# Attention decode: values matmuls in a counted loop on TensorE, one buffer ring for K and V

## Chip, cores and metric

The kernel runs on one core of one Trainium2 chip. The metric is the device time of one execution in microseconds. A profile of one execution shows the engines: PE (TensorE matmuls), PEld (its weight loads), DVE (VectorE), ACT (ScalarE), POOL (GpSimd), SP (the queue that issues the loads), and the DMA transfers.

## The reference: one query per head against 4096 keys

```python
B, H, Sq, Skv, Dh = 8, 32, 1, 4096, 128          # q, k, v in bf16
scale = q.shape[-1] ** -0.5
scores = einsum('bhqd,bhkd->bhqk', q, k) * scale
attn = softmax(scores, axis=-1)
out = einsum('bhqk,bhkd->bhqd', attn, v)
```

There are 256 heads, and each has one query row. K and V are 268 MB each, and every byte of them is used once.

## The kernel before

**Tiles.** A tile t is 8 heads (G) of K or V, and there are 32 tiles (NT). A head's 4096 rows lie on 16 partitions with 256 rows (C) on each, so that a tile of K or V is 128 partitions x 256 rows x 128 numbers, 8.4 MB. Each comes by one DMA (`load`, L139), a few at the two ends of the run in pieces (`cuts`).

**Scores.** `product` (L174) multiplies a quarter of K's rows in place by the query on DVE (L179), and then folds the 128 products to 64 (L182) and, in the first two quarters, to 32 (L187). `sum_over_d` (L194) adds further on PE, by matmuls with an identity, 4 or 8 for a quarter, into one of three PSUM buffers `ps`. `scores_of` (L208) adds the last 8 numbers of each row on DVE (L211). There are four quarters u = 0 to 3 in each tile.

**Weights.** `weights_of` (L218) takes the largest score of the tile's heads, and ACT computes eight exponentials (L240), one for each head's column g: `w[:, c, g]` is the weight of row c in the column of head g, and zero on the partitions of other heads.

**Values.** `values_of` (L250) does 64 matmuls for a tile. Each takes four rows (CB) at once: the stationary operand is w of these rows, 4 x 8 = 32 columns, and the moving operand is 4 x 128 = 512 numbers of V. The 32 output rows go to one of four column groups of PE, `c0 // CB % TG`, so four matmuls in turn write to four quarters of the partitions of `av`. Only the diagonal blocks of the result matter. `copy_of` (L289) copies `av` to SBUF on ACT, and `result_of` (L295) picks the right blocks out of it and adds them up by four matmuls with `pick`, a matrix of zeros and ones that POOL makes at the start (L108 to L123, among the constants). `norm_of`, `recip_of` and `finish_of` divide by the sum of the weights and write out.

**Buffers.** K has two buffers (`k_pool`) and V one (`v_pool`); the last V takes one of K's. So K of tile t+1 waits until K of t-1 is used up, and V of tile t until the values matmuls of t-1 have read V of t-1. The tile framework places all these waits.

**Order.** The order on each engine is written by hand, in the loop at the end (`manual_schedule`). The values matmuls of tile t-1 stand in the middle of tile t, behind the second quarter's sum, with their copy; for the last two tiles they stand behind the fourth quarter's sum. The program is unrolled: every matmul is an instruction of its own, together with a load of its weights.

```python
            if t + 1 < NT:
                load("k", t + 1)
            load("v", t)
            product(t, 0, Q)
            sum_over_d(t, 0)
```

Of the kernel before, what the change touches and what calls it, by code (L numbers as in the profile page):

```python
# [7 lines left out]
ACT = mybir.ActivationFunctionType  # L8
ALU = mybir.AluOpType
AX = mybir.AxisListType  # L10
BF16 = mybir.dt.bfloat16
F32 = mybir.dt.float32

G = 8
KB, VB = 2, 1
TG = 4
R = 2
OB = 4
LAST = 4
NEG = -1.0e30  # L20


@with_exitstack
def kernel(
# [7 lines left out]
    nc = tc.nc  # L32
    B, H, Sq, D = q.shape
    S = k.shape[2]
    P = nc.NUM_PARTITIONS
    assert Sq == 1 and D == 128
    NH = B * H
    PH = P // G
    C = S // PH
    NT = NH // G  # L40
    scale = float(D) ** -0.5
    UC = 64
    DS = 512 // UC
    NU = C // UC
    MC = UC
    CB = 4
    RG = R * G
    NQ = NT // R
    TB = 32
    AG = CB * G  # L50
    assert TG * AG == P and NH % P == 0 and P % G == 0 and TB % PH == 0 and C % CB == 0

    q_n = q.rearrange("b h o d -> (b h o) d").rearrange("(x p) d -> p x d", p=P)
    o_n = out.rearrange("b h o d -> (b h o) d").rearrange("(n u x) d -> n x u d", u=OB, x=RG)
    k_t = k.rearrange("b h s d -> (b h s) d").rearrange("(t p c) d -> t p c d", p=P, c=C)
    v_t = v.rearrange("b h s d -> (b h s) d").rearrange("(t p c) d -> t p c d", p=P, c=C)

    k_pool = ctx.enter_context(tc.tile_pool(name="k_pool", bufs=KB))
    v_pool = ctx.enter_context(tc.tile_pool(name="v_pool", bufs=VB))
    consts = ctx.enter_context(tc.tile_pool(name="consts", bufs=1))  # L60
    q_pool = ctx.enter_context(tc.tile_pool(name="q_pool", bufs=2))
    w_pool = ctx.enter_context(tc.tile_pool(name="w_pool", bufs=2))
    sc_pool = ctx.enter_context(tc.tile_pool(name="sc_pool", bufs=1))
    small = ctx.enter_context(tc.tile_pool(name="small", bufs=2))
    o_pool = ctx.enter_context(tc.tile_pool(name="o_pool", bufs=1))
    ps_s = ctx.enter_context(tc.tile_pool(name="ps_s", bufs=3, space=bass.MemoryType.PSUM))
    ps_v = ctx.enter_context(tc.tile_pool(name="ps_v", bufs=2, space=bass.MemoryType.PSUM))
# [9 lines left out]
        out=ident[:], in_=ident[:], pattern=[[-1, P]], compare_op=ALU.not_equal,  # L77
        fill=1.0, base=0, channel_multiplier=1,
# [31 lines left out]
    for j in range(TG):  # L110
        part = pick[j * AG : (j + 1) * AG, :, :, :]
        nc.gpsimd.affine_select(
            out=part, in_=part, pattern=[[-G, CB], [G, R], [-1, RG]],
            compare_op=ALU.not_equal, fill=1.0, base=0, channel_multiplier=1,
        )
        nc.gpsimd.affine_select(
            out=part, in_=part, pattern=[[-G, CB], [0, R], [0, RG]],
            compare_op=ALU.is_ge, fill=0.0, base=0, channel_multiplier=1,
        )
        nc.gpsimd.affine_select(  # L120
            out=part, in_=part, pattern=[[G, CB], [0, R], [0, RG]],
            compare_op=ALU.is_ge, fill=0.0, base=G - 1, channel_multiplier=-1,
        )  # L123
    ones = consts.tile([P, 1], F32, name="ones")
    nc.vector.memset(ones[:], 1.0)
# [2 lines left out]
    nc.gpsimd.memset(w_last[:], 0.0)  # L128

    loads = {}  # L130
    cuts = {
        ("k", 0): [C // 2] * 2,
        ("k", NT - 3): [C // 2] * 2,
# [4 lines left out]

    def load(kind, t):  # L139
        src = k_t if kind == "k" else v_t  # L140
        home = "v" if kind == "v" and t < NT - 1 else "k"
        pool = k_pool if home == "k" else v_pool
        buf = pool.tile([P, C, D], BF16, name=f"{kind}t", tag=home)
        c0 = 0
        for n in cuts.get((kind, t), [C]):
            nc.sync.dma_start(buf[:, c0 : c0 + n, :], src[t, :, c0 : c0 + n, :])  # L146
            c0 += n
            if kind == "k" and t == 0 and c0 == n:
                nc.sync.dma_start(q_all[:], q_n)
        assert c0 == C  # L150
        loads[kind, t] = buf
# [56 lines left out]
    def scores_of(t, u):  # L208
        if u == 0:
            scs[t] = sc_pool.tile([P, C], F32, name="sc", tag="sc")  # L210
        nc.vector.tensor_reduce(  # L211
            out=scs[t][:, u * UC : (u + 1) * UC], in_=sums.pop((t, u))[:], axis=AX.X, op=ALU.add
        )

    ws = {}
    esums = {}

    def weights_of(t):  # L218
        sc = scs.pop(t)
        pmax = small.tile([P, 1], F32, name="pmax", tag="pmax")  # L220
        nc.vector.tensor_reduce(out=pmax[:], in_=sc[:], axis=AX.X, op=ALU.max)  # L221
        spread = small.tile([P, TB], F32, name="spread", tag="spread")
        nc.vector.tensor_scalar(  # L223
            out=spread[:], in0=same[:], scalar1=pmax[:, 0:1], scalar2=-scale,
            op0=ALU.add, op1=ALU.mult,
        )
        nmax = small.tile([P, 1], F32, name="nmax", tag="nmax")
        nc.vector.tensor_reduce(  # L228
            out=nmax[:], in_=spread[:], axis=AX.X, op=ALU.min, apply_transpose=True
        )  # L230
        bias = small.tile([P, G], F32, name="bias", tag="bias")
        nc.vector.tensor_scalar(  # L232
            out=bias[:], in0=own[:], scalar1=nmax[:, 0:1], scalar2=None, op0=ALU.add
        )
        w = w_pool.tile([P, C, G], BF16, name="w", tag="w")
        if t % R == 0:
            esums[t // R] = small.tile([P, R, G], F32, name="esum", tag="esum")
        esum = esums[t // R]
        for g in range(G):
            nc.scalar.activation(  # L240
                out=w[:, :, g], in_=sc[:], func=ACT.Exp, bias=bias[:, g : g + 1], scale=scale,
                accum_out=esum[:, t % R, g : g + 1],
            )
        ws[t] = w
        if t == NT - 1:
            nc.gpsimd.tensor_copy(out=w_last[:, :, RG - G : RG], in_=w[:, C - LAST : C, :])

    avs = {}

    def values_of(t, lo, hi):  # L250
        vt = loads["v", t]
        w = ws[t]
        if lo == 0:
            avs[t] = ps_v.tile([P, CB * D], F32, name="av", tag="av")
        end = C if t < NT - 1 else C - LAST


        group = [
            0 if t == NT - 1 and C // 2 <= c0 < C // 2 + 3 * C // 16 else c0 // CB % TG
            for c0 in range(0, end, CB)  # L260
        ]
        for c0 in range(lo, hi, CB):
            i = c0 // CB
            j = group[i]
            nc.tensor.matmul(  # L265
                avs[t][j * AG : (j + 1) * AG, :], lhsT=w[:, c0 : c0 + CB, :],
                rhs=vt[:, c0 : c0 + CB, :], start=(i < TG), stop=(j not in group[i + 1 :]),
            )

    ops = {}  # L270
# [16 lines left out]
    combs = {}  # L287

    def copy_of(t):  # L289
        comb = small.tile([P, CB, D], BF16, name="comb", tag="comb")  # L290
        av = avs.pop(t)[:].rearrange("p (m d) -> p m d", d=D)
        nc.scalar.activation(out=comb[:], in_=av, func=ACT.Copy)  # L292
        combs[t] = comb

    def result_of(t):  # L295
        n, r = divmod(t, R)
        comb = combs.pop(t)
        if r == 0:
            ops[n] = ps_o.tile([RG, D], F32, name="op", tag="op")
        if t == NT - 1:  # L300
            for i in range(LAST):
                nc.tensor.matmul(
                    ops[n][:], lhsT=w_last[:, i, :], rhs=loads["v", t][:, C - LAST + i, :],
                    start=False, stop=False,
                )
        for m in range(CB):
            nc.tensor.matmul(  # L307
                ops[n][:], lhsT=pick[:, m, r, :], rhs=comb[:, m, :],
                start=(r == 0 and m == 0), stop=(r == R - 1 and m == CB - 1),
            )  # L310

# [10 lines left out]
            nc.scalar.dma_start(o_n[s, :, lo : u + 1, :], stages[s][:, lo : u + 1, :])  # L322

    Q = C // 4
    load("k", 0)
    with tc.manual_schedule():
        q_prep(0)
        for t in range(NT):
            v_last = t >= NT - 2
            n = t // R - 1  # L330
            if t + 1 < NT:
                load("k", t + 1)
            load("v", t)
            product(t, 0, Q)
            sum_over_d(t, 0)
            if t > 2 and t % R == 1:
                recip_of(n)
                finish_of(n)
            if t + 1 < NT:
                q_prep(t + 1)  # L340
            product(t, Q, 2 * Q)
            sum_over_d(t, 1)
            scores_of(t, 0)
            if t > 0 and not v_last:
                values_of(t - 1, 0, C)
                copy_of(t - 1)
            product(t, 2 * Q, 3 * Q)
            sum_over_d(t, 2)
            scores_of(t, 1)
            product(t, 3 * Q, C)  # L350
            sum_over_d(t, 3)
            scores_of(t, 2)
            if t > 0 and v_last:
                values_of(t - 1, 0, C)
            scores_of(t, 3)
            weights_of(t)
            if t > 0:
                if v_last:
                    copy_of(t - 1)
                if t % R == 0:  # L360
                    norm_of(n)
                result_of(t - 1)
        values_of(NT - 1, 0, C // 2)
        norm_of(NQ - 1)
        recip_of(NQ - 1)
        values_of(NT - 1, C // 2, C - LAST)
        copy_of(NT - 1)
        result_of(NT - 1)
        finish_of(NQ - 1)

# [29 lines left out]
```

## Time and profile before

| | |
|---|---|
| median of 10 runs | 1253.27 us (1252.81 to 1253.87) |
| the profiled execution | 1252.88 us, span 1251.1 us |
| DVE busy | 1038.0 us, 83% |
| PE busy | 504.4 us, 40%, 3067 matmuls |
| ACT busy | 343.8 us, 27% |
| mean granted TensorE clock | 0.635 |
| HBM read | 536.94 MB, 429 GB/s over the span |

The page lists groups of instructions by source line with the number of executions, their busy time and mean, and then the idle time of the engine ahead of them and what ended it. Durations of matmuls overlap, and the busy time of a group counts the overlapped time once. DMA queues are listed with packets, megabytes and the share of the 16 DMA engines' span that they filled. Queues named "instruction" bring the engines' programs.

### The profile page before, as it was taken

What the parts mean: (1) busy time and instruction counts of PE and PEld (TensorE: products, weight loads), DVE (VectorE), ACT (ScalarE), POOL (GpSimd) and SP (SyncE); (2) the same over time, 40 slices, a digit from 0 to 9 for tenths busy, and PEclk for the clock granted to TensorE, in tenths of its full rate; (3) what the DMA queues carried; (4) which work ended last, traced back from release to release, by engine and by line L of the source; (5) the groups of instructions that cost most, each with busy time, mean ns of one, the idle gap of its engine ahead of it and who ended that gap; (6) DMA issues with size and microseconds to landing.
All of it is one profiled execution on the core that took longest, in us unless ns stands there. A gap on an engine that the chain in (4) does not pass through costs nothing.

```text
span 1251.1 us, 7723 instructions
## 1 busy us (share of the span) xinstructions
PE 504.4 (40%) x3067; PEld 176.6 (14%) x3067; DVE 1038.0 (83%) x588; ACT 343.8 (27%) x625; POOL 6.0 (0%) x26
## 2 busy tenths in 40 slices
PE   1344432344333443333533344432444334454455
PEld 0011110111111111111111111111111111111122
DVE  5989898888988889788898888987879888899981
ACT  0321233321233312333123331233321333213333
POOL 1000000000000000000000000000000000000000
PEclk9767655666656666566665666656666556667776
DMA  9999999999999999999999999999999999999997
GB/s 404 436 434 435 436 434 434 434 434 434 434 422 434 436 436 430 430 432 432 437 436 428 435 434 432 424 434 434 436 434 434 437 432 436 432 423 427 429 441 328
DMA packets 11444, 537.50 MB, mean 430 GB/s; under 512 B 1808, under 2 KB 2064, under 8 KB 2320
## 3 DMA queue, kind: packets, MB, share of 16 engines
q1 hardware_dynamic: 11072, 536.94, 99.4%
q8 instruction: 24, 0.39, 0.1%
q10 hardware_dynamic: 336, 0.07, 0.0%
q14 instruction: 12, 0.10, 0.0%
HBM read 536.94 MB, written 0.07 MB: 429 GB/s over the span
## 4 chain that ended last, share of the span: by engine, by line
DMA 76%; PE 14%; DVE 8%; issue 1%; SPq 0%; ACT 0%
DMA vt<-in_v_dram 75%; PE av L265 13%; DVE kt L179 5%; DVE kt L182 2%; PE ps L199 1%; DMA q_all<-in_q_dram 1%; DVE kt L187 0%; DVE sc L211 0%; SPq L146 0%; DVE pmax L221 0%; DVE spread L223 0%; DVE nmax L228 0%; ACT comb L292 0%; PE op L307 0%; ACT stage L316 0%
## 5 line engine op out<-in xcount | busy, mean ns | idle before, releaser
L179 DVE TENSOR_TENSOR kt<-kt,qb 128x8192 bf16<-128x8192 bf16 x128 | 565.1, 4415 | 88.3 <-DMA kt<-in_k_dram 76.8
L199 PE MATMUL ps<-kt,ident 128*128 128x512 bf16 x792 | 295.2, 532 | 661.5 <-DVE kt L187 504.0
L240 ACT ACTIVATE w<-sc,bias 128x256 bf16<-128x256 f32 x256 | 301.0, 1590 | 365.2 <-DVE bias L232 365.2
L182 DVE TENSOR_TENSOR kt<-kt 128x4096 bf16<-128x4096 bf16 x128 | 293.3, 2292 | 4.4
L199 PEld LDWEIGHTS <-ident 128*128 128x128 bf16 x792 | 92.5, 120 | 824.5 <-issue 674.5
L265 PE MATMUL av<-vt,w 128*32 128x512 bf16 x2047 | 181.2, 525 | 43.7 <-DMA vt<-in_v_dram 43.7
L211 DVE TENSOR_REDUCE sc<-ps 128x64 f32<-128x512 f32 x128 | 87.6, 685 | 89.4 <-PE ps L199 89.4
L292 ACT ACTIVATE comb<-av 128x512 bf16<-128x512 f32 x32 | 19.7, 616 | 411.8 <-PE av L265 411.8
L240 ACT ACTIVATION_READ_ACCUMULATOR w<-sc,bias 128x1 f32 x256 | 126.9, 496 | 0.0
L265 PEld LDWEIGHTS <-w 128*32 128x32 bf16 x2047 | 68.0, 127 | 167.8 <-issue 81.4
L187 DVE TENSOR_TENSOR kt<-kt 128x2048 bf16<-128x2048 bf16 x58 | 71.0, 1225 | 2.0
L162 ACT ACTIVATE qg<-qh 8x128 bf16<-8x128 f32 x32 | 8.5, 267 | 93.1 <-PE qh L158 93.1
L307 PE MATMUL op<-comb,pick 128*16 128x128 bf16 x128 | 16.8, 276 | 13.0 <-ACT comb L292 13.0
L221 DVE TENSOR_REDUCE pmax<-sc 128x1 f32<-128x256 f32 x32 | 13.4, 420 | 1.1
L285 DVE RECIPROCAL rz<-zp 16x1 f32<-16x1 f32 x16 | 2.4, 149 | 13.9 <-PE zp L277 13.9
L158 PE MATMUL qh<-q_all,ident 128*8 128x128 bf16 x32 | 8.5, 265 | 13.2 <-DMA q_all<-in_q_dram 13.2
L164 PE MATMUL qp<-qg,heads 8*128 8x128 bf16 x32 | 8.3, 258 | 12.7 <-ACT qg L162 12.7
L307 PEld LDWEIGHTS <-pick 128*16 128x16 bf16 x128 | 9.5, 106 | 25.2 <-issue 25.1
L316 ACT ACTIVATE stage<-op,rz 16x128 bf16<-16x128 f32 x16 | 6.2, 386 | 23.1 <-DVE rz L285 17.0
L166 ACT ACTIVATE qb<-qp 128x128 bf16<-128x128 f32 x32 | 8.9, 278 | 11.0 <-PE qp L164 11.0
L223 DVE TENSOR_SCALAR spread<-same,pmax 128x32 f32<-128x32 f32 x32 | 7.7, 241 | 1.1
L232 DVE TENSOR_SCALAR bias<-own,nmax 128x8 f32<-128x8 f32 x32 | 7.4, 230 | 1.1
(27 smaller groups left out, 26.9 us busy)
## 6 DMA issues: line engine op xcount, KB each, us to landing
kt<-in_k_dram SPq DMA_DIRECT2D x7, 4096.0 KB, 34.2
kt<-in_k_dram SPq DMA_DIRECT2D x2, 2048.0 KB, 36.8
vt<-in_v_dram SPq DMA_DIRECT2D x1, 4096.0 KB, 39.7
vt<-in_v_dram SPq DMA_DIRECT2D x1, 2048.0 KB, 44.2
vt<-in_v_dram SPq DMA_DIRECT2D x1, 1024.0 KB, 46.1
vt<-in_v_dram SPq DMA_DIRECT2D x1, 512.0 KB, 46.9
vt<-in_v_dram SPq DMA_DIRECT2D x31, 33.1
kt<-in_k_dram SPq DMA_DIRECT2D x28, 43.5
```

The costliest lines, as they stand in the source:

```text
L158: nc.tensor.matmul(qh[:], lhsT=ident[:, p0 : p0 + G], rhs=q_all[:, x, :], start=True, stop=True)
L166: nc.scalar.activation(out=qb[:, 0, :], in_=qp[:], func=ACT.Copy)
L179: nc.vector.tensor_tensor(out=part, in0=part, in1=qb[:].to_broadcast([P, MC, D]), op=ALU.mult)
L182: nc.vector.tensor_tensor(out=part[:, :, 0 : D // 2], in0=part[:, :, 0 : D // 2], in1=part[:, :, D // 2 : D], op=ALU.add,)
L187: nc.vector.tensor_tensor(out=part[:, :, 0 : D // 4], in0=part[:, :, 0 : D // 4], in1=part[:, :, D // 4 : D // 2], op=ALU.add,)
L199: nc.tensor.matmul(ps[:], lhsT=ident[:], rhs=kt[:, u * UC : (u + 1) * UC, s * DS : (s + 1) * DS], start=(s == 0), stop=(s == n - 1),)
L211: nc.vector.tensor_reduce(out=scs[t][:, u * UC : (u + 1) * UC], in_=sums.pop((t, u))[:], axis=AX.X, op=ALU.add)
L221: nc.vector.tensor_reduce(out=pmax[:], in_=sc[:], axis=AX.X, op=ALU.max)
L240: nc.scalar.activation(out=w[:, :, g], in_=sc[:], func=ACT.Exp, bias=bias[:, g : g + 1], scale=scale, accum_out=esum[:, t % R, g : g + 1],)
L265: nc.tensor.matmul(avs[t][j * AG : (j + 1) * AG, :], lhsT=w[:, c0 : c0 + CB, :], rhs=vt[:, c0 : c0 + CB, :], start=(i < TG), stop=(j not i ...
L292: nc.scalar.activation(out=comb[:], in_=av, func=ACT.Copy)
L307: nc.tensor.matmul(ops[n][:], lhsT=pick[:, m, r, :], rhs=comb[:, m, :], start=(r == 0 and m == 0), stop=(r == R - 1 and m == CB - 1),)
```

## The change

**Layout of the weights.** w becomes `[P, C // CB, G, CB]`: four rows of one head lie side by side, so that the 32 columns of one values matmul are ordered by head and then by row, and one stretch of 32 numbers serves each matmul. The pattern of `pick` follows and needs one select for each column group in place of three. `w_last`, the copy of the last four rows' weights, is filled through a permuted view.

**Loop.** The values matmuls of all but the last three tiles stand in a new function `values_loop`. The first and last two of the 64 (EDGE) are written out; the other 60 run as ten turns of a loop on PE with six matmuls each (LOOP), whose addresses come from two registers. All 64 write to the first column group, so only 32 partitions of `av` are filled, copied and picked from. A loop is a block of its own in the program: [...]PE waits ahead of it for everything that stands before it in the program. To keep that short, the loop of tile t-1 stands behind the fourth quarter's sum of tile t, and the loads of K t+1 and V t and the fourth reduction of tile t are put behind it in the program (`behind_loop` fixes this order, without a wait). The copy of `av` moves behind the exponentials of tile t.

**Buffers.** K and V share one ring of three buffers. By the order of the loads, K of t+1 takes the buffer of V of t-2, and V of t that of K of t. The score buffer gets a second copy, `comb` loses one.

```diff
-KB, VB = 2, 1
+SLOTS = 3
+LOOP = 6
+EDGE = 2
...
-    k_pool = ctx.enter_context(tc.tile_pool(name="k_pool", bufs=KB))
-    v_pool = ctx.enter_context(tc.tile_pool(name="v_pool", bufs=VB))
+    kv_pool = ctx.enter_context(tc.tile_pool(name="kv_pool", bufs=SLOTS))
...
-    sc_pool = ctx.enter_context(tc.tile_pool(name="sc_pool", bufs=1))
+    sc_pool = ctx.enter_context(tc.tile_pool(name="sc_pool", bufs=2))
...
-            out=part, in_=part, pattern=[[-G, CB], [G, R], [-1, RG]],
+            out=part, in_=part, pattern=[[-1, CB], [CB * G, R], [-CB, RG]],
             compare_op=ALU.not_equal, fill=1.0, base=0, channel_multiplier=1,
-        )
-        nc.gpsimd.affine_select(
-            out=part, in_=part, pattern=[[-G, CB], [0, R], [0, RG]],
-            compare_op=ALU.is_ge, fill=0.0, base=0, channel_multiplier=1,
-        )
-        nc.gpsimd.affine_select(
-            out=part, in_=part, pattern=[[G, CB], [0, R], [0, RG]],
-            compare_op=ALU.is_ge, fill=0.0, base=G - 1, channel_multiplier=-1,
         )
...
+    def behind_loop(made):
+        if loops:
+            tc.add_manual_dep(
+                made.ins, loops[-1].name,
+                mybir.DependencyInfo(
+                    mybir.DependencyClass.NoSync, mybir.DependencyReason.SCHED_ONLY
+                ),
+            )
...
-        home = "v" if kind == "v" and t < NT - 1 else "k"
-        pool = k_pool if home == "k" else v_pool
-        buf = pool.tile([P, C, D], BF16, name=f"{kind}t", tag=home)
+        buf = kv_pool.tile([P, C, D], BF16, name=f"{kind}t", tag="kv")
...
-            nc.sync.dma_start(buf[:, c0 : c0 + n, :], src[t, :, c0 : c0 + n, :])
+            dma = nc.sync.dma_start(buf[:, c0 : c0 + n, :], src[t, :, c0 : c0 + n, :])
+            behind_loop(dma)
...
+        if u == NU - 1:
+            behind_loop(made)
...
-        w = w_pool.tile([P, C, G], BF16, name="w", tag="w")
+        w = w_pool.tile([P, C // CB, G, CB], BF16, name="w", tag="w")
...
+        sc_g = sc[:].rearrange("p (i m) -> p i m", m=CB)
         for g in range(G):
             nc.scalar.activation(
-                out=w[:, :, g], in_=sc[:], func=ACT.Exp, bias=bias[:, g : g + 1], scale=scale,
+                out=w[:, :, g, :], in_=sc_g, func=ACT.Exp, bias=bias[:, g : g + 1], scale=scale,
...
+    def values_loop(t):
+        vf = loads["v", t][:].rearrange("p c d -> p (c d)")
+        wf = ws[t][:].rearrange("p i g m -> p (i g m)")
+        avs[t] = ps_v.tile([P, CB * D], F32, name="av", tag="av")
+        av = avs[t][0:AG, :]
+        nv, nw = CB * D, CB * G
+        def one(i, **how):
+            pe.matmul(
+                av, lhsT=wf[:, i * nw : (i + 1) * nw], rhs=vf[:, i * nv : (i + 1) * nv], **how
+            )
+        with tc.tile_critical() as loop:
+            for i in range(EDGE):
+                one(i, start=(i == 0), stop=False)
+            end = (NV - EDGE) * nw
+            pe.reg_mov(rw, EDGE * nw)
+            pe.reg_mov(rv, EDGE * nv)
+            with pe.While(lambda: pe.snap(rw, min_val=EDGE * nw, max_val=end) < end):
+                ow = pe.snap(rw, min_val=EDGE * nw, max_val=end - LOOP * nw)
+                ov = pe.snap(rv, min_val=EDGE * nv, max_val=(NV - EDGE - LOOP) * nv)
+                for i in range(LOOP):
+                    pe.matmul(
+                        av, lhsT=wf[:, bass.ds(ow + i * nw, nw)],
+                        rhs=vf[:, bass.ds(ov + i * nv, nv)],
+                        start=False, stop=False,
+                    )
+                pe.reg_add(rw, rw, LOOP * nw)
+                pe.reg_add(rv, rv, LOOP * nv)
+            for i in range(NV - EDGE, NV):
+                one(i, start=False, stop=(i == NV - 1))
+        loops.append(loop)
+    LT = NT - 3
...
-        comb = small.tile([P, CB, D], BF16, name="comb", tag="comb")
+        comb = o_pool.tile([P, CB, D], BF16, name="comb", tag="comb")
         av = avs.pop(t)[:].rearrange("p (m d) -> p m d", d=D)
-        nc.scalar.activation(out=comb[:], in_=av, func=ACT.Copy)
+        n = AG if t < LT else P
+        nc.scalar.activation(out=comb[0:n, :, :], in_=av[0:n, :, :], func=ACT.Copy)
...
+            loop = 0 < t <= LT
...
-            if t + 1 < NT:
-                load("k", t + 1)
-            load("v", t)
+            if not loop:
+                if t + 1 < NT:
+                    load("k", t + 1)
+                load("v", t)
...
             scores_of(t, 0)
-            if t > 0 and not v_last:
-                values_of(t - 1, 0, C)
-                copy_of(t - 1)
             product(t, 2 * Q, 3 * Q)
...
             scores_of(t, 2)
-            if t > 0 and v_last:
+            if loop:
+                values_loop(t - 1)
+                load("k", t + 1)
+                load("v", t)
+            if v_last:
                 values_of(t - 1, 0, C)
             scores_of(t, 3)
             weights_of(t)
             if t > 0:
-                if v_last:
-                    copy_of(t - 1)
+                copy_of(t - 1)
```

More of the change, by code (lines that the diff above doesn't have):

```diff
@@ L50 @@
     AG = CB * G
-    assert TG * AG == P and NH % P == 0 and P % G == 0 and TB % PH == 0 and C % CB == 0
+    NV = C // CB
+    assert (NV - 2 * EDGE) % LOOP == 0
+    assert LAST == CB and TG * AG == P and NH % P == 0 and P % G == 0 and TB % PH == 0 and C % CB == 0
     q_n = q.rearrange("b h o d -> (b h o) d").rearrange("(x p) d -> p x d", p=P)
@@ L130 @@
     loads = {}
+    loops = []
+    def behind_loop(made):
[6 more added lines that the diff above has]
+            )
     cuts = {
@@ L210, in scores_of @@
             scs[t] = sc_pool.tile([P, C], F32, name="sc", tag="sc")
-        nc.vector.tensor_reduce(
+        made = nc.vector.tensor_reduce(
             out=scs[t][:, u * UC : (u + 1) * UC], in_=sums.pop((t, u))[:], axis=AX.X, op=ALU.add
         )
+        if u == NU - 1:
+            behind_loop(made)
     ws = {}
@@ L245, in weights_of @@
         if t == NT - 1:
-            nc.gpsimd.tensor_copy(out=w_last[:, :, RG - G : RG], in_=w[:, C - LAST : C, :])
+            nc.gpsimd.tensor_copy(
+                out=w_last[:, :, RG - G : RG].rearrange("p m g -> p g m"),
+                in_=w[:, (C - LAST) // CB, :, :],
+            )
     avs = {}
+    pe = nc.tensor
+    rv = pe.alloc_register("rv")
+    rw = pe.alloc_register("rw")
+    def values_loop(t):
[22 more added lines that the diff above has]
+                        start=False, stop=False,
+                    )
+                pe.reg_add(rw, rw, LOOP * nw)
[4 more added lines that the diff above has]
+    LT = NT - 3
     def values_of(t, lo, hi):
@@ L265, in values_of @@
             nc.tensor.matmul(
-                avs[t][j * AG : (j + 1) * AG, :], lhsT=w[:, c0 : c0 + CB, :],
+                avs[t][j * AG : (j + 1) * AG, :], lhsT=w[:, i, :, :],
                 rhs=vt[:, c0 : c0 + CB, :], start=(i < TG), stop=(j not in group[i + 1 :]),
@@ L305, in result_of @@
                 )
+        e = AG if t < LT else P
         for m in range(CB):
             nc.tensor.matmul(
-                ops[n][:], lhsT=pick[:, m, r, :], rhs=comb[:, m, :],
+                ops[n][:], lhsT=pick[0:e, m, r, :], rhs=comb[0:e, m, :],
                 start=(r == 0 and m == 0), stop=(r == R - 1 and m == CB - 1),
@@ L325 @@
     load("k", 0)
-    with tc.manual_schedule():
+    E = mybir.EngineType
+    with tc.manual_schedule(engines={E.PE, E.DVE, E.Activation, E.SP}):
         q_prep(0)
         for t in range(NT):
+            loop = 0 < t <= LT
             v_last = t >= NT - 2
             n = t // R - 1
-            if t + 1 < NT:
-                load("k", t + 1)
-            load("v", t)
+            if not loop:
+                if t + 1 < NT:
+                    load("k", t + 1)
+                load("v", t)
             product(t, 0, Q)
```

## The prediction

> **What bounds the kernel now.** I read the page first: queues, groups, chain. Then the waits, then the timeline of one middle tile and of the start.
>
> ```profile
> q1 hardware_dynamic: 11072, 536.94, 99.4%
> q8 instruction: 24, 0.39, 0.1%
> ...
> L265 PE MATMUL av<-vt,w 128*32 128x512 bf16 x2047 | 181.2, 525 | 43.7 <-DMA vt<-in_v_dram 43.7
> L211 DVE TENSOR_REDUCE sc<-ps 128x64 f32<-128x512 f32 x128 | 87.6, 685 | 89.4 <-PE ps L199 89.4
> ```
>
> The load queue fills the 16 DMA engines for 99.4% of the span: the kernel is bound by its 537 MB. 64 loads of 8.4 MB take 19.35 us each (a V load lands every 38.7 us in the chain of waits), so a tile has a period of 38.7 us. TensorE fetches its program in 24 transfers, 0.39 MB, so 16 KB each; all values matmuls together are only 181 us.
>
> ```profile
> DVE sc L211 <- PE ps L199: 89.4, 34, 3.1
> ...
> DVE kt L179 <- DMA kt<-in_k_dram: 76.8, 25, 4.3
> ```
>
> VectorE waits in nearly every tile twice: about 3 us for the last sum, about 3 us for the next K. The second is its slack: its own round is 36.0 us of 38.7.
>
> ```profile
> 625.82 4.42 DVE L179 TENSOR_TENSOR kt<-kt,qb 128x8192 bf16<-128x8192 bf16 x1 [2.78 <-DMA kt<-in_k_dram]
> ...
> 641.67 0.68 DVE L211 TENSOR_REDUCE sc<-ps 128x64 f32<-128x512 f32 x1
> ...
> 656.32 3.57 PE L199 MATMUL ps<-kt,ident 128*128 128x512 bf16 x8 [4.04 <-DVE kt L182]
> ...
> 659.90 0.58 PE L307 MATMUL op<-comb,pick 128*16 128x128 bf16 x4
> 659.93 0.33 SPq L146 DMA_DIRECT2D kt<-in_k_dram  x1
> ...
> 664.59 4.43 DVE L179 TENSOR_TENSOR kt<-kt,qb 128x8192 bf16<-128x8192 bf16 x1 [2.72 <-DMA kt<-in_k_dram]
> ```
>
> This is the clock of a tile, counted from its K's arrival: first score reduction at 15.85, last sum done (K's buffer free) at 34.1, next K at 38.7.
>
> ```profile
> 73.45 0.33 SPq L146 DMA_DIRECT2D vt<-in_v_dram  x1
> 84.20 0.33 SPq L146 DMA_DIRECT2D kt<-in_k_dram  x1
> ```
>
> At the start VectorE is late: K of tile 1 landed at 42.2 but is only free at 84.2. V of tile 1 doesn't mind, since it takes V 0's buffer and was issued at 73.45, while K of tile 2 (landing 80.6 to 82.3, by engine) was still coming in.
>
> ```profile
> 606.42 5.90 PE L265 MATMUL av<-vt,w 128*32 128x512 bf16 x64 [1.40 <-DMA vt<-in_v_dram]
> ...
> 1242.62 2.10 PE L265 MATMUL av<-vt,w 128*32 128x512 bf16 x9
> ```
>
> The first line is a tile's 64 values matmuls today, spread over four column groups. The second is nine in a row in one group, at the full clock: the last lasts 0.38, so the other eight are (2.10 - 0.38) / 8 = 0.215 us apart.
>
> [...]64 in 5.90 us are 0.092 each, against 0.215 in one group. [...]the sum of eight takes 3.57 us, 0.43 each, twice 0.215.[...]
>
> **The change, part by part.**
>
> *Nothing or nearly so.* The new layout of w changes only the write stride of the exponentials: even 10% of their 9.2 us per tile is hidden, for they end near 45 of a tile's clock and the copy behind them waits for the loop, until 49 or later; uncovered, it would be 0.9 us per tile. Eight fewer selects on POOL lie in the first 6 us, before any V.[...]
>
> *Buffers: the start.* K(t+1) now takes V(t-2)'s buffer, V(t) takes K(t)'s. In a middle tile V(t) is issued at 34.1 instead of in mid-tile, and its first packets come 1.0 us later (first issue 0.81, first packet 1.83), 3.5 us before the queue runs dry at 38.7: free, but that is all the slack. Behind it on SP stands K(t+2), which waits for the loop. At the start V 1 can't go before 84.2, so the queue is dry from 80.6 to 85.2: +4.6 us, once.
>
> *Fewer instructions.* By the new order, TensorE's program shrinks from 6134 (3067 matmuls and as many weight loads) to about 3780 instructions, 24 fetches to 14. What a fetch costs shows in the sixteen completions of each load: they spread over 0.4 us at 61, 1.8 after the first fetch (75), 3.2 from 509 on and 4.7 at the end[...]. The slowest engine decides, so at most 4.7 us are to be had; with 14 fetches and an even restart at 85 I count one or two rounds, 1.6 to 3.2 left: -1.5 to -3.1 us.
>
> *The loop.* It starts when the last sum is done plus 0.4 us (PE waits for its own sum; the other things that it waits for, VectorE's third reduction, the V load and old ScalarE work, are long past). Behind it on PE stand the result of t-1 and all sums of the next tile; who waits is VectorE's first reduction there. Let X be the loop's time. After it: drain 0.3, copy 0.6, result 0.6, first sum 1.1, together 2.6. From that reduction to the last sum are 34.1 - 15.85 = 18.3. So the ring PE-VectorE has the period X + 0.4 + 2.6 + 18.3 = X + 21.3, hidden as long as X is at most 38.7 - 21.3 = 17.4 us. Beyond, each us of X costs one per period, 28 of them.
>
> X from the array: 64 x 0.215 = 13.8, plus 0.7 for a cold beginning: 14.5, hidden. [...]X = 10 x 1.79 + 4 x 0.215 + 0.4 = 19.2, period 40.5.
>
> **Sum**, against the profiled execution (span 1251.1, time 1252.9): 28 x 1.8 = 50.4, less 2.7 swallowed by VectorE's slack, start +4.6, fetches -3.0 (a queue that runs dry every tile levels the engines) = +49.3. Span 1300, and against the median of 1253.3: 1302 us.
>
> **Rivals.**
> - *Loop hidden* (the other side). If an iteration takes under 1.59 us (0.265 per matmul), X stays under 17.4 and only start and fetches remain: +4.6 less 1.5 to 3.1, so 1255 to 1256.5, middle 1255.6: not slower by what can be told. For: the array needs only 14.5, and the limit is only 11% below my 1.79. Against: 22 sequencer instructions per 6 matmuls, register addresses on 12 of them.
> - *Page stalls.* [...]
> - *Array stays cold.* [...]64 x 0.43 = 27.3, period 48.6 + 0.4, +288, 1540. Against: the second line of matmuls above, warm in one group.
> - *Faster*: only if the start's gap is less than I read and the fetches give their full 4.7: about 1249.
>
> **Numbers.** Sequencer-bound loop 0.44 (own range 1262 to 1400), hidden 0.31, page stalls 0.15, cold 0.04, faster 0.06. Likeliest: 1302. Range 1254 to 1400: it takes in the hidden loop and the page stalls, and leaves out faster, cold[...]. 0.2% is 2.5 us, about what a measurement of this kernel tells from no change. Hidden lies just about there, so 0.20 of its 0.31 goes to same: faster 0.06, same 0.20, slower 0.74.
>
> **What would show it.** The chain of waits would change from the V loads to PE's loop and VectorE; the load queue's share would fall to some 96%; matmuls of the loop would start 0.30 us apart with a longer gap every six; "DVE sc <- PE ps" would grow to 5 us or more a tile and "DVE kt <- DMA kt" shrink. Matmuls 0.22 apart and a queue at 99% with a single gap at 81 to 85 us would show the hidden loop; loops of 30 us among ones of 15, the page stalls; 0.43 apart, the cold array. No gap at 85 us would prove the part on buffers wrong.

## Result and profile after

The changed kernel takes 1299.6 us (median of 8 runs, 1298.64 to 1301.56) against 1253.0 of the kernel before (28 runs, 1252.77 to 1253.9): a ratio of 1.0374, 95% interval 1.0365 to 1.0383, slower by 46.6 us. The forecast was 1302. That figure came out well, but by luck: two errors of opposite sign met in it, as the traces show.

First the page of the changed kernel: two DMA queues (packets, MB, share of the span), then three groups (busy us, mean ns of one, idle time ahead of the group and what ended it).

```profile
q1 hardware_dynamic: 11072, 536.94, 96.6%
q8 instruction: 14, 0.23, 0.1%
...
L288 PE MATMUL av<-vt,w 128*32 x1740 | 423.1, 382 | 9.7 <-issue 0.2
...
L217 DVE TENSOR_REDUCE sc<-ps 128x64 f32<-128x512 f32 x128 | 87.7, 685 | 115.0 <-PE ps L205 115.0
L336 DVE RECIPROCAL rz<-zp 16x1 f32<-16x1 f32 x16 | 2.5, 155 | 71.4 <-PE zp L328 71.4
```

The load queue is no longer full: 96.6% of 1297.2 us, where it was 99.4% of 1251.1. The unfilled part is 44 us against 7.5, so 37 of the 46.6 us stand in it. The instruction fetches are 14, as counted. The last line is one that the forecast doesn't mention: sixteen reciprocals of 16 numbers each, 2.5 us of work, ahead of which VectorE stands idle for 71.4 us.

The waits of the changed kernel (us in total, times, longest), and behind them the wait for the same reciprocal in the kernel before:

```profile
DVE sc L217 <- PE ps L205: 115.0, 47, 4.5
...
DVE rz L336 <- PE zp L328: 71.4, 15, 8.5
...
DVE kt L185 <- DMA kt<-in_k_dram: 38.3, 13, 4.0
```

```profile
DVE rz L285 <- PE zp L277: 13.9, 1, 13.9
```

VectorE's wait for the first sum of a tile, the one that the forecast saw growing to 5 us, is 0.7 to 1.6 us in every second tile and nothing in the others (the 4.5 is one tile at the end of the run; the other waits of that row are for last sums, 3 us as before). Instead it waits 15 times for `zp`, the sum of the weights: 14 times in every second tile, 63 us in all, and once at the end of the run, 8.5 us, where the kernel before waits 13.9. And the wait for the next K, its slack, is left in 13 tiles only. One such tile in the timeline of the changed kernel (start, duration, engine, line; in brackets the idle time before and what ended it):

```profile
683.21 0.33 SPq L151 DMA_DIRECT2D vt<-in_v_dram  x1
...
683.62 1.04 PE L274 MATMUL av<-vt,w 128*32 128x512 bf16 x2 [0.44 <-issue]
...
684.45 14.78 PE L288 MATMUL av<-vt,w 128*32 x60
...
687.22 4.42 DVE L185 TENSOR_TENSOR kt<-kt,qb 128x8192 bf16<-128x8192 bf16 x1 [2.07 <-DMA kt<-in_k_dram]
...
694.01 1.22 DVE L193 TENSOR_TENSOR kt<-kt 128x2048 bf16<-128x2048 bf16 x1
...
700.20 0.19 PE L328 MATMUL zp<-ones,esum 128*16 128x1 f32 x2 [0.20 <-PEq L278]
...
700.42 0.15 DVE L336 RECIPROCAL rz<-zp 16x1 f32<-16x1 f32 x1 [5.20 <-PE zp L328]
700.51 4.39 DVE L185 TENSOR_TENSOR kt<-kt,qb 128x8192 bf16<-128x8192 bf16 x1
...
726.41 0.33 SPq L151 DMA_DIRECT2D vt<-in_v_dram  x1
...
726.82 0.60 PE L274 MATMUL av<-vt,w 128*32 128x512 bf16 x2 [0.44 <-issue]
```

The loop runs from 683.62 to 700.0: 16.4 us, not 19.2. VectorE begins the tile at 687.22, is through with the first quarter at 695.2, and the next instruction in its order is `recip_of`. Its `zp` comes from `norm_of`, which stands on TensorE behind the loop. So VectorE does nothing from 695.2 to 700.42, and the three quarters behind it, the sums that free K's buffer and with them the next V load (726.41) are late by as much. From loop to loop this tile takes 43.2 us, the one before it 37.2; the tiles alternate, and over the 28 periods the mean is 40.12 (first loop at 84.79, last at 1208.15) against the 38.7 that the loads need. 28 x 1.42 = 40 us.

The rest lies at the start. SyncE's queue there in the changed kernel:

```profile
84.38 0.33 SPq L151 DMA_DIRECT2D vt<-in_v_dram  x1
101.23 0.33 SPq L151 DMA_DIRECT2D kt<-in_k_dram  x1
```

V 1 was issued at 84.38, when K 2 had landed at 80.87, and it landed at 106.27. The distance of the two landings is 25.40 us instead of 19.35, so 6.05 are lost. The kernel before loses 1.4 at the same place (81 to 82 us), behind its first instruction fetch, so at V 1 the changed kernel is 4.6 us behind it; but the changed kernel's own first fetch comes one load later and costs 1.3 there, and at the next K it is 5.9 us behind. Together some 46 of the 46.6 us. (Counted by landings, the lag grows from 5.9 there to 43.6 at the last load, and the work behind that load takes 2.5 us longer.)

### The profile page after: what moved, and what is told of

It is laid out like the page before. It is cut to its first block, busy times and chain, and to the rows that moved or that the text cites. A ratio compares the mean times of both kernels' runs of the same rounds, so it can differ in the third digit from the quotient of the medians.

```text
span 1297.2 us, 11039 instructions
## 1 busy us (share of the span) xinstructions
PE 814.1 (63%) x3067; PEld 294.2 (23%) x3067; DVE 1039.9 (80%) x588; ACT 172.4 (13%) x625; POOL 3.3 (0%) x18
## 3 DMA queue, kind: packets, MB, share of 16 engines
q1 hardware_dynamic: 11072, 536.94, 96.6%
## 5 line engine op out<-in xcount | busy, mean ns | idle before, releaser
L185 DVE TENSOR_TENSOR kt<-kt,qb 128x8192 bf16<-128x8192 bf16 x128 | 565.1, 4415 | 50.1 <-DMA kt<-in_k_dram 38.3
L205 PE MATMUL ps<-kt,ident 128*128 128x512 bf16 x792 | 314.1, 561 | 398.3 <-DVE kt L188 302.4
L288 PE MATMUL av<-vt,w 128*32 x1740 | 423.1, 382 | 9.7 <-issue 0.2
L288 PEld LDWEIGHTS av<-vt,w 128*32 x1740 | 165.1, 95 | 269.7 <-issue 147.1
L249 ACT ACTIVATE w<-sc,bias 128x256 bf16<-128x256 f32 x256 | 126.4, 494 | 709.8 <-DVE bias L240 709.8
L344 ACT ACTIVATE comb<-av 32x512 bf16<-32x512 f32 (+1 forms) x32 | 18.8, 587 | 323.7 <-PEq L278 316.0
L336 DVE RECIPROCAL rz<-zp 16x1 f32<-16x1 f32 x16 | 2.5, 155 | 71.4 <-PE zp L328 71.4
L274 PE MATMUL av<-vt,w 128*32 128x512 bf16 x116 | 40.5, 436 | 14.4 <-issue 12.8
L249 ACT ACTIVATION_READ_ACCUMULATOR w<-sc,bias 128x1 f32 x256 | 47.7, 186 | 0.0
L360 PE MATMUL op<-comb,pick 32*16 32x128 bf16 (+1 forms) x128 | 12.3, 215 | 25.3 <-ACT comb L344 25.3
L274 PEld LDWEIGHTS av<-vt,w 128*32 128x32 bf16 x116 | 6.7, 98 | 53.5 <-issue 53.5
L360 PEld LDWEIGHTS <-pick 32*16 32x16 bf16 (+1 forms) x128 | 8.9, 83 | 32.4 <-issue 32.0
L316 PE MATMUL av<-vt,w 128*32 128x512 bf16 x191 | 15.9, 450 | 0.0
L229 DVE TENSOR_REDUCE pmax<-sc 128x1 f32<-128x256 f32 x32 | 13.4, 420 | 1.1
## 6 DMA issues: line engine op xcount, KB each, us to landing
kt<-in_k_dram SPq DMA_DIRECT2D x2, 2048.0 KB, 14.9
```

The costliest lines, as they stand in the source:

```text
L185: nc.vector.tensor_tensor(out=part, in0=part, in1=qb[:].to_broadcast([P, MC, D]), op=ALU.mult)
L205: nc.tensor.matmul(ps[:], lhsT=ident[:], rhs=kt[:, u * UC : (u + 1) * UC, s * DS : (s + 1) * DS], start=(s == 0), stop=(s == n - 1),)
L249: nc.scalar.activation(out=w[:, :, g, :], in_=sc_g, func=ACT.Exp, bias=bias[:, g : g + 1], scale=scale, accum_out=esum[:, t % R, g : g + 1],)
L274: pe.matmul(av, lhsT=wf[:, i * nw : (i + 1) * nw], rhs=vf[:, i * nv : (i + 1) * nv], **how)
L288: pe.matmul(av, lhsT=wf[:, bass.ds(ow + i * nw, nw)], rhs=vf[:, bass.ds(ov + i * nv, nv)], start=False, stop=False,)
L316: nc.tensor.matmul(avs[t][j * AG : (j + 1) * AG, :], lhsT=w[:, i, :, :], rhs=vt[:, c0 : c0 + CB, :], start=(i < TG), stop=(j not in group[ ...
```

## The experiments

Each ran with the kernel before on the same chip (1253.0 to 1253.2 us in all of them). Four came first.

**The reciprocal alone** (e1_recip_late): `recip_of` and `finish_of` go behind the first reduction of the tile.

```diff
             sum_over_d(t, 0)
-            if t > 2 and t % R == 1:
-                recip_of(n)
-                finish_of(n)
...
             scores_of(t, 0)
+            if t > 2 and t % R == 1:
+                recip_of(n)
+                finish_of(n)
```

> The changed kernel with the reciprocal and the final scaling (every second tile) moved from behind the first quarter to behind the second quarter's first score reduction. Theory A, the reciprocal: VectorE stands about 5 us in every second tile at the reciprocal, because the matmul it waits for lies behind the loop; without that the 16.3 us loop is hidden (17.4 are), and only the start's gap is left: 1254 to 1258 us, no wait left at the reciprocal, tiles 38.7 us apart. Theory B, the ring loop-to-first-sum is too long after all: VectorE waits the same 3 us per pair at the first reduction instead, and the time stays at 1290 to 1300. Theory C, the shared buffers issue V too late in any case: stays above 1285, with the queue dry in every tile.

Measured: 1266.55 us, ratio 1.0111 (1.0094 to 1.0128). Two steps of the order, moved by one quarter of a tile, bring back 33 of the 46.6 us. The same place in the timeline of this kernel:

```profile
668.66 14.77 PE L288 MATMUL av<-vt,w 128*32 x60
...
684.40 0.19 PE L328 MATMUL zp<-ones,esum 128*16 128x1 f32 x2 [0.19 <-PEq L278]
...
687.82 0.68 DVE L217 TENSOR_REDUCE sc<-ps 128x64 f32<-128x512 f32 x1
...
688.42 0.15 DVE L336 RECIPROCAL rz<-zp 16x1 f32<-16x1 f32 x1
```

The loop is as long as before (14.77 us for 60 matmuls, 14.78 in the changed kernel), and the reciprocal has no bracket any more: `zp` was there nearly 4 us ahead of it. The mean period is 38.84 us. Still 13.4 us remain, more than the 5.9 of the start, and the time lies outside what each of the three theories gave.

**A longer loop** (e2_long_loop): e1 with two matmuls in a turn.

```diff
-LOOP = 6
+LOOP = 2
```

> As the run with the late reciprocal, but two matmuls per turn in place of six, 30 turns in place of 10. A turn's end costs 0.205 us in the changed kernel's trace, so the loop should take 13.8 + 0.7 + 29 x 0.2 = 20.4 us if the cost is one per turn. By the prediction's ring (period = loop + 21.3) the period is then 41.7, 3.0 us over 38.7 in 28 tiles: about 1335 us. If the limit of 17.4 us was wrong and up to 21 are hidden, it stays at 1255 to 1260.

Measured: 1548.77 us, ratio 1.235 (1.2329 to 1.2371). TensorE in the timeline of this kernel, three turns out of thirty, and the wait that has grown:

```profile
720.16 0.60 PE L288 MATMUL av<-vt,w 128*32 x2 [0.30 <-issue]
721.02 0.60 PE L288 MATMUL av<-vt,w 128*32 x2 [0.26 <-issue]
721.91 0.60 PE L288 MATMUL av<-vt,w 128*32 x2 [0.29 <-issue]
```

```profile
DVE sc L217 <- PE ps L205: 457.4, 61, 16.8
```

A turn takes 0.86 to 0.89 us, mean 0.877, and the loop 27.45. The expected 20.4 rested on wrong prices of the turn. The period is 48.4 us (median; most lie within 0.2 of it): that is X + 20.9, where the forecast had worked out X + 21.3. So the ring from loop to loop through VectorE's first reduction exists and has the length that was read from the profile before; in the changed kernel it just isn't the one that decides. With six in a turn the turn takes 1.501 us (five steps of 0.216 and one of 0.421). A straight line through n = 2 and n = 6 puts a turn of n matmuls at 0.565 + 0.156 n us; where nothing else holds them up, n matmuls take 0.216 n. The two cross between n = 9 and n = 10.

**No loop** (e3_unrolled): the changed kernel, the same place, buffers and column group, the 64 matmuls written out, the reciprocal where the change has it.

```diff
-        with tc.tile_critical() as loop:
-            for i in range(EDGE):
-                one(i, start=(i == 0), stop=False)
...
+        for i in range(NV):
+            one(i, start=(i == 0), stop=(i == NV - 1))
```

> The changed kernel with the loop written out: the same 64 matmuls in one column group, in the same place, with the same buffers and the early reciprocal, but no loop, no registers, no block of its own. Theory A (the place of the reciprocal behind the values): still slower than before, as the values take 14.6 us and the reciprocal waits 3 us or more in every second tile: 1265 to 1285, 24 program fetches. Theory L, loop control is what costs: back to 1254 to 1258.

Measured: 1271.13 us, ratio 1.0136 (1.0119 to 1.0153), with 64 matmuls in 14.0 to 15.1 us. A loop control that costs 1.2 to 2.3 us a tile is worth 28 us; the other 18 are there without any loop. The tiles alternate here too (41.1 and 37.4 us in the mean), for `zp` stands behind the values as before.

**The layout alone** (e4_layout): the kernel before with the new order of the weights' columns and the picking to match.

```diff
-        w = w_pool.tile([P, C, G], BF16, name="w", tag="w")
+        w = w_pool.tile([P, C // CB, G, CB], BF16, name="w", tag="w")
...
-                out=w[:, :, g], in_=sc[:], func=ACT.Exp, bias=bias[:, g : g + 1], scale=scale,
+                out=w[:, :, g, :], in_=sc_g, func=ACT.Exp, bias=bias[:, g : g + 1], scale=scale,
...
-                avs[t][j * AG : (j + 1) * AG, :], lhsT=w[:, c0 : c0 + CB, :],
+                avs[t][j * AG : (j + 1) * AG, :], lhsT=w[:, i, :, :],
```

> The kernel before with the new layout of the weights alone (exponentials, pick and the values matmuls' column order to match; no loop, old buffers and order). The exponentials should take 0.49 us in place of 1.59, as in the changed kernel, which shows that the layout does that; the time stays within 1 us of 1253, since ScalarE is not what the kernel waits for. If the faster exponentials were due to the loop's order instead, they stay at 1.59.

Measured: 1253.22 us, ratio 1.0 (0.9991 to 1.0009). The exponentials on the page of the kernel before, and then of this one:

```profile
L240 ACT ACTIVATE w<-sc,bias 128x256 bf16<-128x256 f32 x256 | 301.0, 1590 | 365.2 <-DVE bias L232 365.2
```

```profile
L233 ACT ACTIVATE w<-sc,bias 128x256 bf16<-128x256 f32 x256 | 126.3, 494 | 367.2 <-DVE bias L224 367.2
```

An exponential takes 0.494 us instead of 1.590, and nothing of it reaches the end: ScalarE waits 367 us for the bias as it waited 365 before, and the queue is as full. This half of the change is real and worth nothing here.

Now the 13 us that e1 keeps.

**The start** (e5_start): e1 with the buffers, and the values in mid-tile, of the kernel before for tiles 0 to 2; loop and ring of three begin with tile 4. (The lines that choose the buffers are left out here.)

```diff
-            loop = 0 < t <= LT
+            loop = FIRST <= t <= LT
...
+            if 0 < t < FIRST:
+                values_of(t - 1, 0, C)
+                copy_of(t - 1)
```

> As e1, but values of tiles 0 to 2 are written out in mid-tile with the buffers of the kernel before; the loop and the ring of three begin with tile 4. Theory A (13 us are left in e1: some 6 at the start, some 7 in the ring, whose loads have only 2 us of slack): the queue no longer runs dry at 80 to 85 us and the time falls by 5 to 7 us, to 1259 to 1262. Theory B (the start's gap is refilled later, what is left lies in the loop): within 2 us of e1's 1266.6.

Measured: 1258.31 us, ratio 1.0047 (1.003 to 1.0063). SyncE's queue at the start in this kernel:

```profile
72.91 0.33 SPq L162 DMA_DIRECT2D vt<-in_v_dram  x1
84.33 0.33 SPq L162 DMA_DIRECT2D kt<-in_k_dram  x1
```

V 1 is issued 9 us ahead of K 2's landing instead of 3.5 behind it, and the gap is gone: at the landing of K 3 e5 is level with the kernel before (0.2 us ahead), where e1 is 5.5 behind it. 8.2 us came back between the medians (5.1 between the two profiled executions; e1's four runs lie up to 6 us apart). Beyond the start the traces show one thing more: at 397.64 e1 entered its loop 3.7 us late, just after a store of the result had landed (issued at 376.4, 20.5 us under way), and the lag of its loads grew by 2.6 us there. In e5 that store landed in time.

**Ten in a turn** (e6_ten_per_turn): the changed kernel with `LOOP = 10`, a reading of the sum from e2.

> The changed kernel with ten matmuls in a turn (six turns for ten), the reciprocal where it was. Theory A (a turn costs the sequencer 0.565 + 0.156 n us, worked out from n = 2 and n = 6, against 0.216 n in the array, so that ten are hidden): no wider gap at the turn's end, loop 14.5 to 14.8 us, and the time that of the unrolled e3, 1268 to 1276. Theory B (each turn costs the array 0.2 us whatever its length): loop 15.6 to 15.9, time 1285 to 1294.

Measured: 1272.06 us, ratio 1.015 (1.0133 to 1.0167). The timeline of this kernel:

```profile
674.00 13.20 PE L288 MATMUL av<-vt,w 128*32 x60
...
687.82 0.19 PE L328 MATMUL zp<-ones,esum 128*16 128x1 f32 x2 [0.19 <-PEq L278]
```

60 matmuls in 13.20 us, no step over 0.22 at a turn's end: the loop takes 14.2 us (median; 14.1 to 14.9), as short as the unrolled one, and the time is the unrolled one's, with 16 instruction fetches against 24. The tiles with a reciprocal take 41.0 us here and 43.2 in the changed kernel; less the loop's 14.2 and 16.4 that is 26.8 both times. So there are two rings: X + 20.9 in a tile without a reciprocal, X + 26.8 (up to 27 in other tiles) in one with it.

**Both** (e7_start_ten): e5 with ten in a turn.

> e5 with ten matmuls in a turn. Theory A (with the reciprocal moved, the ring's period is hidden either way): within 2 us of e5, at most 3 us less through the 1.6 us of slack that V gains. Theory B (what is left over the time before is the loop's length): 5 us or more below e5.

Measured: 1257.25 us, ratio 1.0031 (1.0017 to 1.0045); the intervals of e5 and e7 overlap. With the reciprocal moved, a loop 2 us shorter buys some 1 us, within the noise. In the trace the landings of e7 lose 7.1 us in pieces of 0.3 to 1.6, where the distance of two exceeds 19.35; those of the kernel before lose 4.2, each time behind an instruction fetch.

**The loop in mid-tile.** If the ring's small slack is what is left, the loop at the old place with the old buffers should be free (e8_mid_one_group).

```diff
             scores_of(t, 0)
+            if loop:
+                values_loop(t - 1)
+                load("k", t + 1)
+                load("v", t)
+                copy_of(t - 1)
...
-    kv_pool = ctx.enter_context(tc.tile_pool(name="kv_pool", bufs=SLOTS))
+    k_pool = ctx.enter_context(tc.tile_pool(name="k_pool", bufs=KB))
+    v_pool = ctx.enter_context(tc.tile_pool(name="v_pool", bufs=VB))
```

> The loop of ten in one column group, but in mid-tile as the values of the kernel before, with its buffers (two for K, one for V). The loads then have 10 us of slack or more. Theory A (what e1 keeps is the ring's small slack, the loop itself costs the queue nothing): 1249 to 1255, below the kernel before if the fewer instruction fetches show. Theory B (the loop itself, its fetches or its registers, costs 5 us or more wherever it stands): 1258 or more.

Measured: 1316.41 us, ratio 1.0491 (1.045 to 1.0531): a miss of both theories, and of my count of the slack. The timeline of this kernel:

```profile
524.44 1.04 PE L277 MATMUL av<-vt,w 128*32 128x512 bf16 x2 [2.23 <-PEq L281]
...
540.09 0.33 SPq L154 DMA_DIRECT2D vt<-in_v_dram  x1
...
542.04 0.69 DVE L222 TENSOR_REDUCE sc<-ps 128x64 f32<-128x512 f32 x1 [7.23 <-PE ps L210]
```

A wait of this kernel (us in total, times, longest):

```profile
PE av L277 <- DMA out_dram<-stage: 19.9, 3, 12.5
```

V landed at 523.33, the loop holds its only buffer until 540.0, and the next V is issued 2.6 us before K's landing at 542.66. In the kernel before, four column groups do the same work in 5 to 6 us and the buffer comes free some 13 us ahead. And the third quarter's sums stand behind the loop, so VectorE waits 7.2 us where it has about 3 to spare. One column group takes two and a half to three times as long as four (15.5 us here), and in this place, with these buffers, there is no room for that. Three loops were besides entered late for a store of the result, which values matmuls don't read: 19.9 us in all.

**V in halves** (e9_v_halves): each half of V has its own buffer and its own loop of 1 + 30 + 1 matmuls, behind the first and the second quarter's sums.

```diff
+            if loop:
+                values_loop(t - 1, 0)
+                load("k", t + 1)
+                load("v", t, 0)
             product(t, Q, 2 * Q)
             sum_over_d(t, 1)
             scores_of(t, 0)
+            if loop:
+                values_loop(t - 1, 1)
+                load("v", t, 1)
+                copy_of(t - 1)
```

> e8 mended where its trace shows the loss: V comes in two halves with a buffer each, and the loop is cut in two (1 + 3 x 10 + 1 matmuls, one column group), the first half behind the first quarter's sums, the second behind the second quarter's. In e8 the one V buffer came free 16 us after its landing and the third quarter's sums came 7 us late. Theory A (the loop itself costs the queue nothing; what the ring versions keep is a load that comes a little too late): each half is freed 8 us after its loop begins, VectorE waits no more than before, 1249 to 1254; at the lower end if the fewer instruction fetches show, against 1253.0 of the kernel before. Theory B (a loop of registers on TensorE costs some 4 us over the run wherever it stands, as e7 still has over the kernel before): 1256 to 1260.

Measured: 1373.96 us, ratio 1.0965 (1.095 to 1.098), again a miss of both theories. The second loop's entry in the timeline of this kernel:

```profile
594.82 1.02 PE L222 MATMUL ps<-kt,ident 128*128 128x512 bf16 x4 [0.19 <-PEq L297]
...
599.89 0.39 PE L292 MATMUL av<-vt,w 128*32 128x512 bf16 x1 [4.05 <-DMA kt<-in_k_dram]
```

These matmuls read no K at all: that load (landed at 599.11) is the next tile's, and it only stands ahead of the loop in the program. In the whole run 15 such entries wait 74 us for a K load, three wait 39 us for a store, and 25 wait up to 0.9 us each for the next tile's query. So entering a loop waits for what the program has ahead of it on other queues and engines, whether the loop needs it or not. In the changed kernel nothing of that kind stands there, because its loads were put behind the loop; the stores in e1 and e8 were such cases.

**Nothing ahead that isn't needed** (e10_loads_behind): e9 with the loads, the next query and the store moved behind the loops (the lines of the query and the store are left out here).

```diff
                 values_loop(t - 1, 0)
-                load("k", t + 1)
-                load("v", t, 0)
+                load("v", t - 1, [1])
...
                 values_loop(t - 1, 1)
-                load("v", t, 1)
+                load("k", t + 1)
+                load("v", t, [0])
                 copy_of(t - 1)
```

> e9 with nothing put ahead of a loop that the loop doesn't need. In the trace of e9 TensorE enters the second loop of a tile only when the K load that stands ahead of it in the program has landed (4 to 6 us), and the first one when the query of the next tile is made: entering a loop waits for all that was issued ahead of it on every engine and queue. So the loads of K and of V's first half go behind the second loop, V's second half behind the first loop of the next tile, the query and the store of the result behind the second loop. Theory A (e9 lost its time by these waits, the loop itself costs the queue nothing): the K wait is gone, VectorE waits under 3 us a tile for sums, 1249 to 1254. Theory B (a loop costs a fixed amount at its entry and end wherever it stands, two of them per tile twice that): above 1260.

Measured: 1255.82 us, ratio 1.0022 (1.0013 to 1.0031), 118 us below e9. It lies between the two theories, nearer to A. Two waits of this kernel:

```profile
DVE sc L234 <- PE ps L222: 95.2, 59, 4.1
...
DVE kt L200 <- DMA kt<-in_k_dram: 76.1, 26, 3.7
```

VectorE waits about as in the kernel before (89.4 and 76.8 us there). Counted as for e7, with 9.71 us as the usual distance of two half loads, the landings of e10 lose 4.3 us in pieces of 0.4 to 1.2, each where an instruction fetch (of TensorE or another engine) went by; the kernel before loses 4.2. So the loop itself costs the queue nothing that these traces show. The ring versions, then, would pay for V loads that come a little too late: most of theirs are issued some 4.4 us ahead of the last landing, those of e10 by 12 or more. No run changed that lead alone.

And yet e10 is 2.8 us slower than the kernel before. The same load lands 0.05 us later than there at 62 us of the span, 0.9 at 606 and 2.4 at 1169: a drift, not a gap. It goes with the halves of V. Two halves take 2 x 9.714 = 19.43 us, a whole K in the same trace 19.36; over 31 loads of V that is 2.1 of the 2.8 us. In the kernel before, a K that comes in halves takes 9.72 + 9.71 us as well, against 19.36 for a whole one. No version that ran is faster than the kernel before.

## Why the forecast came out near, and where it was wrong

- *Bound, period, nothing for the layout.* Right (e4: 1.0). That the exponentials would change by 10% at most was wrong, they take a third; it was hidden either way. The old order writes one 2-byte number per 16 bytes and takes 1.590 us, the new one writes four side by side and takes 0.494; why that is so, no run shows.
- *The start.* The place and the reason are right (e5). The gap is 6.05 us and not 4.6, since a load issued to an empty queue takes 21.9 us from issue to landing where a full one delivers every 19.35: 2.5 us of lead are needed, not the 1.0 to the first packet. In the trace of the changed kernel the 2.5 us of V 1 lie mostly ahead: its first packet starts 0.96 us after the issue, the first packets of the 16 engines take up to 3.4 us where 2.42 is usual, and the landing comes 0.3 us behind the end of the last packet. At the next K the changed kernel is 5.9 us behind the kernel before, so this term was too small by 1.3. The same 2.5 us make the slack of the middle tiles some 2 us instead of 3.5, and as the completions of a load on the 16 engines lie some 2 us apart there, the engines that finish first have hardly any left. That would be what e1, e5 and e7 go on paying in pieces.
- *Fetches.* 14 as counted. The gain of 3.0 us was not seen by itself: the sixteen completions of a load end 1.7 us apart at 1200 us instead of 4.8, but the queue lost more in gaps than that.
- *The loop's time X*: the first term that was mis-sized. A turn was put at 1.79 us, an estimate of mine that no trace had shown, and takes 1.50; X is 16.3 and not 19.2. By its parts the runs give 156 ns for a weight load, a matmul and their register arithmetic, and 565 ns once per turn. In the trace of the changed kernel a register instruction between the matmuls (L288) takes 74 ns, and each branch of the loop (L284) 71 to 346 ns, 163 in the median.
- *The ring*, the step that failed: "who waits is VectorE's first reduction there". It is X + 21.3 as written, confirmed at X = 27.45 (e2: X + 20.9). From the loop's end to the tile's first sum the changed kernel takes 2.2 us (700.0 to 702.2), where the forecast had 2.6. But behind the loop stands also `norm_of`, and VectorE meets its reciprocal in every second tile ahead of the second quarter, 8 us earlier than that reduction. In those tiles the ring is X + 26.8. A pair of tiles then takes 2X + 47.7, which at X = 16.3 is 80.3 us for the 77.4 that four loads need; measured 80.4 (median). By the forecast's ring alone X = 16.3 would have been hidden, and the loop's 50.4 us zero. The pair alone is not the whole account: at the X of e6, 14.2, it gives 76.1 us, less than four loads need, and e6 still takes 78.6 a pair. In its long tiles (41 us) V is issued only 2.2 to 4.2 us ahead of the last landing, and the queue loses up to 2.4 us there that the short tiles don't win back.
- *So the sum.* The forecast had 50.4 for the loop by too long a loop in too loose a ring; the runs have 40 from a shorter loop in a tighter ring. Two errors of opposite sign met, and the figure is luck. e1 shows the ring's share (33 us without touching the loop), e6 the loop's (27.5 us without touching the ring): either remedy takes most of the loss, since each brings the pair to the four loads or near them.
- *The rivals.* The hidden loop had X right (under 17.4) and the time wrong, for want of the same reciprocal; with it moved and the start mended it is nearly there (e5, 1258.31 against 1255.6). The cold array is out: the loops run at 216 ns a matmul, except for one to five at the beginning of each (mostly 0.30 to 0.43 us apart). Page stalls, loops held up at their turns by instruction fetches, which no trace had shown, are out for the changed kernel: no step between two matmuls in its 29 loops is over 0.58 us. The faster case is out: nothing that ran is faster.
- *What would show it.* The queue's share (96% forecast, 96.6% measured) and the smaller wait for K (38.3 us for 76.8) came as written; 0.30 us a matmul (0.25 measured), and 5 us at the first reduction, did not. Those two told that the time was near for another reason. (The chain on the page of the changed kernel covers only 5% of its span and can't tell.)

## What to carry to other kernels

When a long piece of work is put into an engine's order, list everything that stands behind it there, and for each piece the earliest point where another engine asks for it: a matmul of 0.2 us whose reader comes early in its own order can set the period, and moving that reader is the cheapest cure. A loop on TensorE, as these programs build it, also has an entry that waits for whatever was issued ahead of it (4 us for a K load in e9), so loads, stores and small products that it doesn't need belong behind it. And a transfer is hidden only if it is issued ahead of the queue's last landing by at least what an empty queue costs in all (2.5 us here), not by the time to its first packet (1.0).

## What the runs showed that I had not expected

- With the exponentials' shorter writes the read of the accumulator behind each shrank too, from 0.496 to 0.186 us, though it moves one number per partition either way.
- A turn of a loop on TensorE with n register-addressed matmuls takes the larger of 0.565 + 0.156 n and 0.216 n us: 0.877 at n = 2, 1.501 at 6; at 10 no gap is left.
- One of the 29 loops of e2 took 32.20 us instead of 27.45, its turns 1.03 us instead of 0.88. What sets it apart wasn't tried.
